# One issuing engine for the token transfers of the first unit, and a new hand-written order of 1382 steps, in a delta-rule attention + multiplicative FFN kernel

## The chip, the core and the metric

The kernel runs on one core of one Trainium2 chip. TensorE (PE) multiplies, VectorE (DVE), ScalarE (ACT) and GpSimd (POOL) do the elementwise work, SyncE (SP) issues nearly all transfers, and each engine runs its own instructions strictly in the order in which the program lists them. The metric is the device time of one execution in microseconds (us).

## The reference

```python
# q, k, v: (4, 8, 768, 48), beta: (4, 8, 768); w1, w2: (384, 1024), w3: (1024, 1024), w_out: (1024, 384)
k_n = k / (norm(k) + 1e-6);  state = 0
for t in range(768):
    y[:, :, t] = q_t @ state
    state += beta_t * outer(k_n_t, v_t - k_n_t @ state)
x = y as (4*768 tokens, 384)
out = ((x @ w1) * (x @ w2)) @ w3 @ w_out
```

## The kernel before, in words

The sequence is cut into 12 chunks `c` of 64 tokens; two chunks make a unit `u` (0 to 5), and one unit is 512 tokens over the four batches. The recurrence inside a chunk is solved with the inverse of a triangular 64x64 matrix, of which the two 32x32 diagonal blocks are inverted column by column on DVE. `w3 @ w_out` is folded into one matrix `w34` while the first unit is prepared, and the FFN of a unit runs on PE between the small products of the following chunks.

The program is written as generators; each `yield` ends a step. `ORDER` names one generator per word, and a word runs the next step of that generator. So the table alone sets the order of the instructions on every engine, across all parts. The generators that matter here:

- `k`, `q`, `v`: loads of a chunk. `g`, `N`: squares of the keys and their norms (`g` ends, and `N` ends, with a small product `across`, line 286, that swaps halves). `K`, `Q`: keys or queries transposed on PE (line 369) and copied to `KQ`.
- `s`: scores of a chunk (lines 409 for chunks 0 and 1, 451 and 457 later) and on DVE their products `U` and `PT`; `h`: query scores of chunks 0 and 1 (line 400); `u`: `U` sent to `Ud` in DRAM (line 491).
- `V0` to `V5`: the inversion for a unit. POOL clears `Vb`, the matrix `Ub` comes by a DVE transpose (unit 0, line 505) or from `Ud` (line 510); for units 0 and 1 ACT copies `Vb` in two halves into a PSUM tile `ps_w` (line 518); then come 31 steps of two DVE instructions (lines 524, 529). `V0` ends with four DVE transposes of 2 us (line 533).
- `e`: corner of the inverse (lines 563 to 646). `c`: the chain of chunk `c`, which is product, `R`, product, `X`, product, state `S` (PE line 672, DVE lines 706, 717, 738). `y`: outputs of a chunk (PE line 777), four ACT copies into `xT` (line 795), and the transfers of line 807 that lay the last heads over the free rows of `xT`.
- `P0` to `P35`: a piece of the weights: a transfer (line 837), two ACT conversions (845, 848), a DVE shift (850) and a POOL addition (852), which makes float32 out of float64. `t`: transpose of a piece of `w3` (PE 903, ACT 906); `f`: one fold (PE line 912, ACT 919) in two halves.
- `b` (first chunk of unit 0), `a` (the rest; `a02` is unit 0, column block 2): `x @ w1`, `x @ w2` (line 933), `ab` on ACT and DVE. `S`, `o`, `x`: sums, the last product (line 1165) and the results.

For the first unit the transfers of line 807 are issued per chunk: three for each half of the rows (`e` is 0 or 1). Those of `e == 1` are issued by ACT, all others by SP. An SP or ACT transfer waits for the landing of the eighth transfer before it, since eight completion semaphores go round.

Of the kernel before, what the change touches and what calls it, by code (L numbers as in the profile page):

```python
# [40 lines left out]
g0 N0 N0 P12 V0 P8 P8 P3 P3 P8 s1 P9 P9 Q1 s0 s0 P13 N0 P13 P3 P1 P9 t0 s1 s1 P0 P13 t4 V0 P1 V0
P2 P2 Q1 Q1 h1 P9 t4 P10 V0 P1 P3 P13 V0 P2 t5 P4 P6 V0 V0 P1 P2 t1 V0 P10 P10 P10 P4 P4 t0 V0
f0 V0 P5 V0 t2 P6 P5 P4 P6 P7 P5 t5 V0 P7 P7 P5 P7 f2 q0 t1 P18 V0 V0 V0 P11 P18 P18 V0 V0 P19
P6 P22 P18 f0 P11 P11 V0 P11 V0 f0 V0 V0 t2 f2 P19 P19 V0 t3 P16 f2 t3 P17 V0 t10 P22 P19 Q0 P23
t10 P16 f1 Q0 P22 f1 q2 P16 V0 V0 V0 Q0 P17 P17 P23 P23 f1 t11 V0 P17 t11 P23 P15 P14 h1 P15 q3
P21 f5 f5 P16 V0 V0 V0 V0 t8 f5 t8 h1 P20 P26 P22 t14 t14 h0 t9 P14 V0 V0 P15 P15 t7 t7 k2 V0
P21 t15 f4 t9 f4 P27 V0 V0 t15 v0 V0 P14 P14 t6 k3 Q2 V0 P26 t6 V0 f4 e0 P21 h0 P21 P28 f3 Q2 h0
e0 e0 e0 P20 K2 e1 e0 P26 P26 e0 Q2 g1 f7 n0 e1 e1 g1 g1 e0 g1 P27 P20 e1 n0 P28 P28 c0 c0 f7 e1
y0 g1 P25 P20 P29 v1 g1 g1 c0 y0 c0 P27 P27 n1 K2 K2 y0 y0 f3 f3 c1 P28 f7 n1 t12 K3 K3 t13 t12
f6 t13 P25 K3 P29 Q3 Q3 Q3 Q3 e1 e1 K2 P33 K2 P33 P25 g1 P25 g1 f6 c1 P24 c1 g1 N1 P33 c1 P33  # L50
P35 s2 P35 f6 P34 s2 s2 s2 P29 P29 s2 s2 P30 y1 y1 P34 s3 b6 b6 P34 P34 s3 P24 P35 s3 s3 Q3 P31
P31 b4 b4 s3 c1 u2 u3 N1 Q0 P35 P24 P24 y1 y1 b4 P30 V1 V1 c1 P31 b6 b6 N1 s3 k4 g2 b4 b3 b3 P32
P30 b5 b5 b5 b5 v2 P31 P30 V1 V1 a02 a04 V1 V1 V1 V1 b7 V1 V1 V1 V1 V1 b7 a04 a02 v3 a06 a06 V1
b1 b1 a07 a03 V1 V1 V1 V1 a03 V1 T T P32 c2 P32 P32 V1 k5 a01 a01 a07 V1 V1 a05 b0 n2 b0 a04 a04
V1 a02 a02 a05 V1 V1 T V1 b2 V1 V1 a07 b2 a07 V1 V1 a00 a03 a00 V1 V1 T V1 a03 V1 V1 a06 a00 a06
b3 b1 b3 a00 V1 b0 b1 g2 g2 g2 b0 S0 K3 a01 b7 n2 c2 g2 g2 g2 V1 K3 p4 b7 p4 V1 b2 b2 a05 a01 o0
x0 g2 e2 e2 e2 e2 e3 a05 d4 S0 n3 S0 d4 p5 S0 S0 o0 g2 e2 S0 o0 e3 e2 c2 c2 e3 e3 n3 o0 S0 c2 S0
g2 c2 e3 c3 e3 N2 c3 x0 x0 S0 Q1 S0 d4 S0 d4 o0 y2 p5 c3 S0 x0 o0 y2 V2 S0 c3 S0 y3 d5 d5 S0 y3
x0 x0 x0 x0 s4 s4 d5 d5 s4 s4 s4 s4 s5 s5 s5 s5 s5 s5 y3 S0 N2 u4 u5 c3 c3 x0 o0 x0 x0 a14 a14
a14 a17 a17 N2 a14 a15 a15 V2 V2 V2 V2 V2 V2 V2 V2 V2 a16 a13 a13 V2 V2 V2 V2 a16 V2 v5 V2 p6  # L60
a10 V2 a10 p6 V2 a11 V2 V2 a11 k7 V2 a12 V2 V2 V2 V2 a11 V2 V2 a10 a12 V2 V2 V2 v4 V2 V2 V2 a11
a10 S1 d6 d6 c4 k6 g3 g3 a12 a13 a12 d6 a15 a15 V2 e4 a17 e5 e4 e4 n4 n4 c4 g3 a16 p7 g3 g3 g3
a17 g3 d6 a13 e4 e4 g3 g3 g3 a16 S1 o1 e4 c4 e5 e5 p7 e5 o1 S1 c4 c4 c4 n5 S1 n5 e5 x1 N3 o1 S1
c5 S1 c5 e5 S1 y4 S1 k8 o1 y4 d7 d7 d7 S1 S1 S1 d7 x1 g4 s7 s7 s7 s7 s7 s7 N3 S1 S1 s6 s6 s6 s6
s6 S1 s6 g4 c5 x1 c5 u7 u6 V3 S1 o1 V3 x1 y5 y5 y5 o1 x1 x1 N3 c5 c5 x1 k9 x1 v7 V3 V3 V3 V3 V3
S1 o1 x1 x1 V3 V3 V3 V3 V3 x1 c6 V3 V3 a24 V3 V3 V3 V3 a24 a24 a24 V3 V3 a27 a27 a27 V3 V3 a27
a22 a22 a20 a22 V3 V3 p8 p8 V3 V3 g4 a22 V3 V3 a26 a20 V3 a20 V3 V3 V3 a26 V3 a26 a20 S2 a21 v6
n6 a26 g4 g4 g4 d8 d8 g4 g4 d8 a25 a25 a25 n6 a21 a21 V3 e6 e6 c6 a25 e6 d8 s8 g4 p9 e6 e6 e6 g4
N4 s8 s8 n7 a23 a23 e7 e7 p9 a21 S2 a23 e7 e7 c6 a23 o2 o2 e7 e7 x2 c6 y6 c6 S2 o2 x2 c6 y6 V4
S2 o2 c7 x2 d9 d9 d9 S2 d9 S2 S2 s8 n7 c7 c7 S2 S2 S2 S2 v8 s8 s8 S2 S2 o2 c7 y7 x2 u8 o2 s9 x2  # L70
x2 s9 y7 y7 s9 s9 s9 u9 x2 S2 S2 S2 o2 V4 v9 a30 c7 x2 x2 x2 N4 a31 a31 a30 a32 a32 N4 p10 V4 V4
p10 a35 V4 V4 V4 a36 V4 V4 V4 a33 a33 V4 V4 a37 V4 V4 V4 a36 V4 V4 V4 V4 V4 V4 x2 V4 V4 V4 n8
a35 V4 a34 a34 a34 a37 V4 a33 a31 V4 V4 V4 V4 V4 V4 V4 c7 k10 a34 d10 a33 k11 V4 e8 d10 a30 a30
S3 a36 a36 a31 a35 s9 e8 Q1 c8 g5 g5 g5 e8 e8 d10 a35 g5 n8 c8 a37 a37 e8 e9 e8 e9 a32 a32 e9 c8
g5 g5 g5 o3 e9 c8 n9 n9 p11 g5 g5 g5 v10 S3 S3 V5 e9 e9 c8 S3 S3 S3 o3 x3 o3 x3 x3 d10 c8 c9 c9
S3 S3 S3 y8 y8 c9 c9 o3 p11 s10 y9 N5 N5 o3 S3 S3 S3 S3 s10 S3 d11 d11 W s10 s10 x3 S3 o3 d11
d11 y9 y9 s10 s10 x3 x3 u10 x3 s11 s11 s11 s11 s11 S3 n10 x3 s11 o3 u11 a46 V5 v11 a46 x3 x3 c9
n10 a47 c9 W a47 N5 K0 a42 V5 V5 V5 V5 V5 V5 a42 a40 a40 V5 V5 a43 a44 a44 W Q0 V5 a41 a41 V5 V5
V5 V5 V5 V5 V5 V5 V5 V5 V5 V5 a45 a43 a45 V5 V5 V5 a44 a44 a43 V5 V5 V5 V5 V5 a45 a41 V5 V5 a41
a43 x3 a40 a45 a40 S4 S4 a42 a42 a46 c10 V5 e10 e10 e10 a47 c10 e10 e10 o4 e10 c10 e11 e11 a47  # L80
a46 K1 e11 o4 S4 S4 c10 S4 c10 S4 S4 S4 S4 c10 S4 x4 S4 e11 e11 e11 o4 W x4 n11 c11 n11 W y10
c11 S4 S4 S4 y10 o4 c11 o4 c11 y11 x4 x4 o4 x4 S4 S4 y11 x4 o4 y11 x4 x4 a50 x4 x4 a51 X5 X5 X5
a52 a50 a50 a50 a50 a50 a50 a50 a50 a50 a50 X5 a50 a50 a50 a50 a50 x4 a50 a50 a50 a51 a51 a50
a50 a51 a51 a51 a51 a51 a51 a51 a51 a51 a51 W a51 a51 a51 a51 a51 a51 a51 W a51 W a52 a52 a52
a52 a52 a52 a52 a52 a52 a52 a52 a52 a52 a52 a52 a52 a52 a52 a52 a53 a53 a52 a53 a53 a53 a53 a53
a53 a53 a53 a53 a53 a53 a53 a53 a53 a53 a53 a53 o5 x5 a53 a53 o5 o5 S5 S5 Q2 Q2 S5 o5 x5 x5 S5
o5 S5 S5 o5 S5 x5 S5 o5 x5 K0 x5 x5 x5 x5 x5 x5 K1 x5 x5 x5
"""


# [1 line left out]
def kernel(  # L92
# [651 lines left out]
    def outputs(c):  # L744
# [55 lines left out]
        if u == 0 or cc == 1:  # L800
            cs = slice(cc, cc + 1) if u == 0 else slice(0, 2)
            for e in range(2):
                dma = act.dma_start if u == 0 and e else sync.dma_start
                for j in range(KM):
                    g = C * e + D
                    s = C * e + 16 * j
                    dma(out=xT[g : g + 16, j, :, cs], in_=xT[s : s + 16, NP - 1, :, cs])
# [550 lines left out]
```

## Time and profile before

| | |
|---|---|
| time, median of 3 runs | 562.68 us (562.05 to 563.88) |
| the profiled execution, its own time | 564.32 us |
| its span, first to last instruction | 562.6 us |
| outside the span | 1.7 us |
| PE busy | 535.5 us, 95% |
| DVE, POOL, ACT busy | 342.8, 169.4, 145.7 us |
| mean granted TensorE clock | 0.993 |
| transfers | 54.21 MB, 96 GB/s over the span, 0.9 and more of the DMA engines' time in the first 60 us |

The profile is of one execution, read on one core. Busy time of PE counts a matmul from its start to a modelled end. An idle stretch is written in square brackets, with the event that ended it behind the arrow; "issue" there means that the engine waited for nothing that the profile shows. A matmul of float32 appears as two PE instructions.

### The profile page before, as it was taken

What the parts mean: (1) busy time and instruction counts of PE and PEld (TensorE: products, weight loads), DVE (VectorE), ACT (ScalarE), POOL (GpSimd) and SP (SyncE); (2) the same over time, 40 slices, a digit from 0 to 9 for tenths busy, and PEclk for the clock granted to TensorE, in tenths of its full rate; (3) what the DMA queues carried; (4) which work ended last, traced back from release to release, by engine and by line L of the source; (5) the groups of instructions that cost most, each with busy time, mean ns of one, the idle gap of its engine ahead of it and who ended that gap; (6) DMA issues with size and microseconds to landing.
All of it is one profiled execution on the core that took longest, in us unless ns stands there. A gap on an engine that the chain in (4) does not pass through costs nothing.

```text
span 562.6 us, 19911 instructions
## 1 busy us (share of the span) xinstructions
PE 535.5 (95%) x8732; PEld 392.9 (70%) x8732; DVE 342.8 (61%) x800; ACT 145.7 (26%) x291; POOL 169.4 (30%) x213
## 2 busy tenths in 40 slices
PE   5689999899999999999999999999999999989997
PEld 4556667788888644698544798444986447988897
DVE  6799746469727489555895543796364973213553
ACT  3577755432131020120011220111210202212210
POOL 6565443427370002450003430004640002722000
PEclk9999999799999999999999999999999999999999
DMA  9899957587433674543645314745325012010001
GB/s 200 303 297 244 154 115 158 110 152 90 91 48 62 133 103 95 79 75 83 133 62 105 47 34 83 136 96 86 58 43 123 26 53 42 19 57 1 0 2 56
DMA packets 191526, 54.21 MB, mean 96 GB/s; under 512 B 178928, under 2 KB 185072, under 8 KB 191440
## 3 DMA queue, kind: packets, MB, share of 16 engines
q1 hardware_dynamic: 188848, 52.46, 46.8%
q8 instruction: 68, 1.11, 0.9%
q10 hardware_dynamic: 2592, 0.49, 0.6%
q14 instruction: 18, 0.15, 0.1%
HBM read 41.78 MB, written 9.96 MB: 92 GB/s over the span
## 4 chain that ended last, share of the span: by engine, by line
PE 84%; DVE 10%; issue 4%; DMA 1%; ACT 1%; POOL 0%; ACTq 0%; DVEq 0%
PE ps_f L933 37%; PE ps_f L1165 20%; PE ps_w L672 6%; PE ps_w L777 5%; PE ps_f L1073 4%; PE ps_w L619 3%; PE ps_w L1073 2%; PE ps_f L912 2%; DVE tb L524 2%; DVE ps_w L529 2%; PE ps_w L451 1%; PE ps_f L369 1%; PE ps_w L457 1%; DVE TT L533 1%; DMA ktok<-in_k_dram 1%
## 5 line engine op out<-in xcount | busy, mean ns | idle before, releaser
L1006 POOL TENSOR_TENSOR ab<-ab 128x256 f32<-128x256 f32 x80 | 56.0, 728 | 204.5 <-DVE ab L949 199.0
L933 PE MATMUL ps_f<-xT,w1s 128*128 128x512 f32 (+1 forms) x288 | 108.3, 529 | 0.0
L933 PE MATMUL ps_f<-xT,w2s 128*128 128x512 f32 (+1 forms) x288 | 107.0, 523 | 0.0
L933 PEld LDWEIGHTS ps_f<-xT,w1s 128*128 128x128 f32 x288 | 54.8, 193 | 45.6 <-issue 41.1
L933 PEld LDWEIGHTS ps_f<-xT,w2s 128*128 128x128 f32 x288 | 54.2, 190 | 46.2 <-issue 42.8
L945 ACT COPY ab<-ps_f 128x512 f32<-128x512 f32 (+1 forms) x48 | 23.6, 516 | 137.8 <-PE ps_f L933 125.1
L1165 PE MATMUL ps_f<-w,ab 128*128 128x192 f32 x320 | 56.8, 331 | 1.8 <-DVE osb L1196 1.8
L1165 PEld LDWEIGHTS ps_f<-w,ab 128*128 128x128 f32 x320 | 51.6, 190 | 3.0 <-issue 2.1
L524 DVE TENSOR_TENSOR tb<-Vb,Ub 128x31 f32<-128x31 f32 (+15 forms) x124 | 43.1, 347 | 9.8 <-DMA Ub<-Ud 5.8
L912 PE MATMUL ps_f<-wo,w3T 128*128 128x384 f32 x128 | 43.8, 492 | 1.6 <-ACT w3T L906 1.6
L529 DVE TENSOR_TENSOR Vb<-Vb,tb 128x31 f32<-128x31 f32 (+15 forms) x124 | 42.5, 343 | 4.3
L1165 PE MATMUL ps_f<-room,ab 128*128 128x192 f32 x240 | 42.9, 332 | 0.2 <-ACT osb L1202 0.2
L949 DVE TENSOR_TENSOR ab<-ab,ps_f 128x512 f32<-128x512 f32 (+1 forms) x48 | 27.6, 589 | 22.9 <-PE ps_f L933 22.7
L1165 PEld LDWEIGHTS ps_f<-room,ab 128*128 128x128 f32 x240 | 38.6, 190 | 1.1 <-issue 0.3
L912 PEld LDWEIGHTS ps_f<-wo,w3T 128*128 128x128 f32 x128 | 23.4, 190 | 16.5 <-ACT w3T L906 1.8
L301 POOL TENSOR_TENSOR sq<-ktok 128x384 f32<-128x384 f32 x24 | 19.8, 834 | 49.4 <-DMA out_dram<-osb 24.6
L635 ACT COPY T<-ps_w 32x512 f32<-32x512 f32 x24 | 13.8, 575 | 71.6 <-PE ps_w L619 64.2
L795 ACT COPY xT<-ps_w 112x256 f32<-112x256 f32 x48 | 14.3, 384 | 64.5 <-PE ps_w L777 61.7
L1196 DVE TENSOR_TENSOR room<-room,ps_f 128x384 f32<-128x384 f32 (+1 forms) x13 | 7.0, 535 | 28.6 <-PE ps_f L1165 28.6
L451 PE MATMUL ps_w<-KQ 48*64 48x128 f32 x320 | 21.9, 281 | 2.0 <-DVE PT L474 1.4
L717 DVE TENSOR_TENSOR X<-ps_w,wt 128x768 f32<-128x768 f32 x12 | 11.5, 957 | 20.0 <-PE ps_w L672 17.6
L524 DVE TENSOR_TENSOR tb<-ps_w,Ub 128x31 f32<-128x31 f32 (+15 forms) x62 | 21.0, 339 | 4.2 <-ACT ps_w L518 1.6
(170 smaller groups left out, 806.8 us busy)
## 6 DMA issues: line engine op xcount, KB each, us to landing
vtok<-in_v_dram SPq DMA_DIRECT2D x24, 192.0 KB, 4.5
out_dram<-osb SPq DMA_DIRECT2D x23, 192.0 KB, 2.2
ktok<-in_k_dram SPq DMA_DIRECT2D x44, 96.0 KB, 3.6
raw<-in_moe_w_dram SPq DMA_DIRECT2D x8, 512.0 KB, 6.9
raw<-in_moe_w_dram SPq DMA_DIRECT2D x18, 192.0 KB, 4.8
raw<-in_moe_w_out_dram SPq DMA_DIRECT2D x7, 384.0 KB, 4.9
...
```

Of the source, the lines that this page charges most:

```text
L451: pe.matmul(ps[half(z), 0, n : n + 128], lhsT=x[:, 0, :], rhs=x.rearrange("p j t -> p (j t)"), start=True, stop=True,)
L524: dve.tensor_tensor(out=tv, in0=V[:, 0 : s + 1, s : s + 1].to_broadcast([P, s + 1, n]), in1=U[:, s, s + 1 : BS].unsqueeze(1).to_broadcast( ...
L529: dve.tensor_tensor(out=o, in0=o, in1=tv, op=ALU.subtract)
L672: pe.matmul(out(ps, r, h, z), lhsT=lhs(r, h, z), rhs=rhs(r, h, z), start=True, stop=True,)
L777: i = pe.matmul(region(h, z, r), lhsT=lhs, rhs=rhs, start=part[n] not in part[:n], stop=part[n] not in part[n + 1 :],)
L912: pe.matmul(ps[:, 0:DM], lhsT=w3Ts[jc, kc // 4][:, kc % 4 * P : kc % 4 * P + P], rhs=wo(kc), start=(kc == 0), stop=(kc == KF - 1),)
L933: pe.matmul(ps[:].rearrange("p b c t -> p b (c t)"), lhsT=w[:, m, js], rhs=x[:, m, :, c0:c1].rearrange("p b c t -> p b (c t)"), start=(m = ...
L945: act.copy(out=t, in_=ps)
L949: dve.tensor_tensor(out=t, in0=t, in1=ps, op=ALU.mult)
L1006: (dve if u == last else pool).tensor_tensor(out=o_, in0=x_, in1=y_, op=op)
L1073: pe.matmul(ps[:, j, :], lhsT=w[j], rhs=x, start=first and j == 0, stop=j == 1, skip_group_check=not first,)
L1165: pe.matmul(ps[b][:, b, :], lhsT=ab_of(u, HF * f + i, t0), rhs=ws_[w][:, i], start=first and i == 0 and (b == 0 or n == "F"), stop=i == HF ...
```

## The change

The first part: in the first unit the `e == 1` half of the transfers of line 807 (line 806 after) is issued by SP too. The second part: `ORDER` holds the same 1382 words in another order. No arithmetic, tile, buffer or shape is changed, but since buffers are taken in rotation, a step that comes earlier may take another one.

```diff
         if u == 0 or cc == 1:
             cs = slice(cc, cc + 1) if u == 0 else slice(0, 2)
             for e in range(2):
-                dma = act.dma_start if u == 0 and e else sync.dma_start
                 for j in range(KM):
                     g = C * e + D
                     s = C * e + 16 * j
-                    dma(out=xT[g : g + 16, j, :, cs], in_=xT[s : s + 16, NP - 1, :, cs])
+                    sync.dma_start(
+                        out=xT[g : g + 16, j, :, cs], in_=xT[s : s + 16, NP - 1, :, cs]
+                    )
                 if u == 0 or e:
                     yield
```

The first line of the table, before and after:

```diff
-k0 g0 k1 K0 K0 g0 P12 K0 g0 beta P0 g0 g0 g0 P8 K1 K1 g0 P12 g0 P12 P0 P0 q1 beta beta K1 g0 s0
+k0 g0 g0 g0 K0 V0 g0 k1 P12 K0 K0 beta K1 P0 g0 g0 K1 K1 g0 q1 P12 g0 P12 P12 beta g0 g0 beta N0
```

The first place is the start of PE's program. The rows are the transposes of the keys (line 369), `beta`, the small products of line 286 (`ss` from `g0`, `wt` from `N0`), the scores of chunks 0 and 1 (line 409), the queries, and the first transposes of `w3` (line 903, after the change 904). Before:

```order
L369 MATMUL ps_f<-ident,ktok 48x64 x64
L1257 MATMUL ps_f<-ident,beta_fm 128x16 x12
L286 MATMUL ps_f<-ss,ident 64x16 x2
L409 MATMUL ps_w<-KQ 32x64 x64
L286 MATMUL ps_f<-wt,ident 64x16 x2
L409 MATMUL ps_w<-KQ 32x64 x64
L369 MATMUL ps_f<-ident,X 48x2x32 x32
```

And in the same place after:

```order
L369 MATMUL ps_f<-ident,ktok 48x64 x64
L1258 MATMUL ps_f<-ident,beta_fm 128x16 x12
L286 MATMUL ps_f<-ss,ident 64x16 x2
L409 MATMUL ps_w<-KQ 32x64 x128
L369 MATMUL ps_f<-ident,X 48x2x32 x32
L904 MATMUL ps_f<-ident,w_276 128x128 x4
L904 MATMUL ps_f<-ident,w_289 128x128 x4
```

The product of `wt`, which needs the end of `N0` on DVE, no longer stands between the scores of the two chunks; it now follows the query scores and the third transpose of `w3`.

The second place is on ACT, where the two copies of `Vb` into `ps_w` (line 518) stand; `w3` and `wo` rows are weight conversions, `KQ` rows copies of queries, `w3T` rows copies of a transposed piece of `w3` (`w3T_564` before and `w3T_497` after are the first one that a fold needs). Before:

```order
L518 COPY ps_w_101<-Vb_342 128x512
L845 ACTIVATE wo_223<-spare_114 128x384
L848 ACTIVATE spare_114<-spare_114 128x384
L379 COPY KQ_182<-ps_f_99 112x8x64
L379 COPY KQ_182<-ps_f_93 112x8x64
L906 COPY w3T_522<-ps_f_97 128x512
L518 COPY ps_w_101<-Vb_342 128x512
L845 ACTIVATE w3_556<-kperm_91 128x512
L848 ACTIVATE kperm_91<-kperm_91 128x512
L845 ACTIVATE wo_223<-raw_537 128x384
L848 ACTIVATE raw_537<-raw_537 128x384
L906 COPY w3T_564<-ps_f_95 128x512
```

And after:

```order
L846 ACTIVATE w3_428<-raw_426 128x512
L849 ACTIVATE raw_426<-raw_426 128x512
L518 COPY ps_w_101<-Vb_162 128x512 x2
L846 ACTIVATE wo_283<-raw_438 128x384
L849 ACTIVATE raw_438<-raw_438 128x384
L379 COPY KQ_178<-ps_f_97 112x8x64
L379 COPY KQ_178<-ps_f_99 112x8x64
L846 ACTIVATE w3_487<-kperm_91 128x512
L849 ACTIVATE kperm_91<-kperm_91 128x512
L846 ACTIVATE wo_283<-spare_114 128x384
L849 ACTIVATE spare_114<-spare_114 128x384
L907 COPY w3T_497<-ps_f_93 128x512
```

The second copy now follows the first at once, ahead of the query copies and of every copy that waits for a transpose of `w3`.

The third place is SP's queue around the second chunk's transfers of line 807 (806 after). `Ud` is the store for the second inversion, `Ub` its load, `kperm<-in_moe_w2` the last weight piece. Before:

```order
L491 DMA Ud_1810<-U_106 32x16x32 x8
L807 DMA xT_1294<-xT_1294 16x4x64 x3
L510 DMA Ub_1838<-Ud_1810 128x1024
L233 DMA ktok_1850<-in_k_dram 64x8x48 x4
L837 DMA kperm_91<-in_moe_w2_dram 48x1024
L837 DMA kperm_91<-in_moe_w2_dram 16x1024
```

And after:

```order
L491 DMA Ud_1752<-U_106 32x16x32 x8
L806 DMA xT_1296<-xT_1296 16x4x64 x3
L510 DMA Ub_1842<-Ud_1752 128x1024
L806 DMA xT_1296<-xT_1296 16x4x64 x3
L838 DMA kperm_91<-in_moe_w2_dram 48x1024
L838 DMA kperm_91<-in_moe_w2_dram 16x1024
```

The three transfers that ACT issued now stand behind the load of `Ub`, which waits for the last `Ud` to land. The words of the table from the last half of `s3` on show what PE does meanwhile, up to `a02`, the first user of the second chunk's `xT` (in `b4 b4` the first word is PE's, the second ACT's, and so on):

```diff
-b4 b4 s3 c1 u2 u3 N1 Q0 P35 P24 P24 y1 y1 b4 P30 V1 V1 c1 P31 b6 b6 N1 s3 k4 g2 b4 b3 b3 P32 P30 b5 b5 b5 b5 v2 P31 P30 V1 V1 a02
+s3 s3 s3 Q0 P30 P30 c1 b4 b4 P24 P24 u3 P24 y1 b5 b5 b5 V1 P26 y1 V1 b5 P31 V1 P32 b6 b6 P31 b4 b0 b0 c1 b3 b4 b3 b7 V1 V1 b7 V1 V1 a02
```

More of the change, by code (lines that the diff above doesn't have):

```diff
@@ L39 @@
 ORDER = """
-k0 g0 k1 K0 K0 g0 P12 K0 g0 beta P0 g0 g0 g0 P8 K1 K1 g0 P12 g0 P12 P0 P0 q1 beta beta K1 g0 s0
[L41 to L87, printed above, removed]
+k0 g0 g0 g0 K0 V0 g0 k1 P12 K0 K0 beta K1 P0 g0 g0 K1 K1 g0 q1 P12 g0 P12 P12 beta g0 g0 beta N0
@@ new lines @@
+P8 P9 P8 P8 P8 P3 P0 P3 P3 P9 P0 s1 s1 s1 P9 s0 P3 P0 P13 P13 P13 s0 s0 V0 V0 V0 P1 P1 Q1 P1 P9
+Q1 P10 P13 V0 V0 Q1 P1 P10 P2 P2 t0 t0 P2 P4 P4 V0 t1 P2 t1 V0 P4 P4 h1 t4 t4 N0 P6 f0 P7 P10
+P10 P5 t2 t5 P18 V0 V0 P11 P6 V0 P6 P6 N0 P16 P19 V0 P7 P7 P5 P5 P5 q0 V0 t5 h1 P18 f2 P11 V0
+P18 P7 t2 V0 f0 P14 h1 P22 P18 P19 f0 V0 P11 V0 V0 P11 P19 V0 V0 V0 P16 P16 P17 f2 f2 t10 t10
+P23 Q0 Q0 t3 P19 t11 V0 P16 Q0 V0 t3 P22 P22 P22 P14 V0 V0 V0 f1 V0 V0 P23 P21 t8 P15 f1 P14 t11
+P17 P17 f5 f5 V0 V0 f1 V0 V0 P17 t8 P15 V0 h0 V0 V0 P14 f5 P26 t6 P23 P20 V0 q2 P27 k2 t6 t9 t14
@@ new lines @@
+t9 v0 V0 P23 f4 f4 t14 f4 t15 t15 P21 P15 P15 t7 q3 V0 v1 Q2 Q2 V0 e0 h0 h0 e0 Q2 g1 e0 g1 t7 g1
+f3 e0 e0 K2 P27 K2 e1 e0 e0 n0 e1 k3 f7 P27 n0 e1 c0 e1 P21 e1 f7 V1 g1 c0 y0 P28 c0 P20 P25 f7
+P20 P20 P29 f3 P33 y0 n1 n1 P21 g1 c0 c1 y0 g1 g1 K2 f3 P28 P28 P28 P34 c1 t13 t13 t12 t12 P25
+P27 K3 K3 K3 e1 s2 g1 P25 P29 P35 g1 P25 P33 f6 f6 P29 P29 e1 g1 N1 Q3 Q3 c1 y0 s2 s2 s2 P34 c1
+s2 s2 f6 Q3 s3 K2 P30 P34 P34 P26 P26 P24 y1 y1 s3 P30 P31 N1 P33 N1 s3 b6 b6 P33 P35 P35 u2 P35
+s3 s3 s3 Q0 P30 P30 c1 b4 b4 P24 P24 u3 P24 y1 b5 b5 b5 V1 P26 y1 V1 b5 P31 V1 P32 b6 b6 P31 b4
@@ new lines @@
+b0 b0 c1 b3 b4 b3 b7 V1 V1 b7 V1 V1 a02 V1 a02 V1 a03 V1 a05 V1 k4 V1 a00 V1 V1 P32 P32 a03 V1
+b1 a00 a05 V1 V1 V1 V1 a04 V1 b1 c2 P32 P31 a04 a04 a04 a01 a01 T T T v2 n2 a02 T V1 k5 a07 a07
+V1 v3 a02 V1 V1 a03 a03 V1 V1 V1 V1 V1 V1 a06 a06 b2 V1 b2 a07 a07 V1 a01 V1 V1 V1 a01 p4 p4 b2
+n3 V1 V1 b2 a00 a00 a05 a05 g2 g2 g2 g2 a06 n2 b1 b1 b0 e2 b0 a06 g2 b3 b3 b7 b7 o0 g2 c2 n3 x0
+e2 e2 g2 g2 o0 d4 e2 g2 e2 g2 o0 S0 S0 S0 e2 c2 d4 S0 S0 e3 S0 S0 x0 S0 S0 S0 S0 e3 e3 S0 S0 d4
+p5 c2 c2 e3 c2 x0 S0 o0 c3 S0 e3 c3 o0 e3 N2 y2 c3 x0 o0 d4 p5 y2 S0 c3 y3 x0 x0 x0 d5 d5 s4 s4
@@ new lines @@
+o0 x0 y3 s4 s4 d5 d5 s4 s4 N2 s5 y3 u4 s5 V2 s5 s5 s5 N2 s5 c3 u5 V2 x0 p6 x0 a14 p6 a14 a14 a14
+a13 a13 V2 V2 V2 V2 V2 a12 a12 V2 a16 a16 V2 V2 V2 V2 V2 V2 V2 a15 V2 a15 a11 a11 V2 V2 V2 V2 V2
+V2 V2 V2 V2 v5 x0 V2 a10 V2 V2 k6 V2 v4 V2 V2 V2 V2 a17 a17 a15 a15 a10 k7 d6 d6 d6 a10 a10 c3
+S1 n5 n4 a13 a12 a12 a13 V2 e4 a17 e4 a11 g3 g3 g3 g3 a11 Q3 c4 g3 g3 n4 c4 e4 a16 a16 e5 e4 e4
+e4 o1 x1 S1 a17 S1 S1 S1 e5 e5 S1 e5 d6 n5 g3 c4 c4 g3 o1 S1 c4 V3 c4 g3 e5 e5 o1 p7 g3 N3 c5 p7
+x1 S1 x1 S1 y4 S1 y4 c5 o1 d7 d7 d7 d7 s7 s7 k8 g4 s7 s7 s6 s7 s7 u7 s6 s6 s6 s6 s6 c5 S1 c5 o1
@@ new lines @@
+u6 y5 S1 x1 V3 o1 S1 x1 x1 c5 S1 y5 y5 S1 x1 V3 k9 S1 g4 c5 x1 x1 p8 V3 V3 V3 V3 V3 o1 c6 x1 V3
+V3 N3 N3 V3 V3 V3 V3 V3 V3 a27 a27 a25 x1 g4 a20 a25 a20 V3 V3 a25 a25 p8 a22 a22 V3 a24 a21 g4
+V3 V3 V3 a24 V3 d8 d8 p9 v6 V3 V3 a21 g4 g4 V3 V3 V3 V3 V3 V3 V3 V3 a22 a22 a27 a27 a20 n6 a20
+V3 e6 g4 a26 a26 a26 a24 d8 a21 n6 c6 e6 a26 d8 e7 a24 e6 e6 p9 g4 g4 g4 s8 N4 s8 a23 a23 s8 e6
+S2 e7 a21 e6 a23 a23 c6 e7 e7 c6 v7 o2 v9 o2 n7 n7 S2 y6 S2 S2 S2 V4 x2 K2 N4 c6 c6 o2 y6 e7 S2
+S2 S2 d9 d9 p10 S2 e7 c7 S2 x2 o2 d9 d9 c7 S2 s8 c7 x2 s8 o2 s8 c7 S2 y7 S2 v8 n8 x2 K1 o2 x2 x2
@@ new lines @@
+u8 Q2 s9 s9 S2 S2 s9 y7 y7 s9 s9 u9 S2 o2 x2 s9 c7 x2 c7 V4 a32 a32 N4 k10 x2 x2 a36 a36 d10 d10
+V4 a30 a30 V4 V4 a33 a35 Q1 V4 a37 V4 V4 V4 V4 a33 V4 V4 c8 V4 V4 V4 V4 a35 a37 V4 V4 V4 k11 a34
+n9 a34 a31 p10 V4 V4 V4 V4 a34 V4 V4 V4 V4 x2 V4 V4 V4 V4 V4 V4 V4 e8 a31 d10 a31 a31 a35 a34 V5
+a33 a30 a30 a36 n8 c8 K3 e8 e8 a35 a37 a33 a36 e8 K3 e8 e8 a37 a32 e9 e9 e9 p11 e9 c8 a32 o3 x3
+S3 S3 g5 g5 g5 g5 n9 g5 S3 c8 d10 S3 S3 S3 c8 e9 p11 g5 g5 g5 o3 o3 e9 c8 c9 x3 x3 S3 S3 g5 g5
+c9 y8 y8 K1 S3 S3 c9 c9 o3 N5 o3 x3 s10 d11 s10 s10 y9 s10 s10 d11 d11 d11 S3 S3 W y9 y9 S3 S3
@@ new lines @@
+o3 x3 W s10 x3 x3 s11 s11 s11 s11 s11 u10 u11 V5 S3 S3 x3 x3 o3 x3 x3 a44 s11 v11 V5 a45 V5 V5
+V5 V5 a45 a42 a42 v10 V5 a44 a46 a46 V5 V5 V5 V5 V5 V5 a41 V5 V5 V5 V5 a43 c9 a43 V5 V5 a41 a47
+a47 V5 V5 a44 a44 V5 V5 V5 V5 W V5 a40 a40 a45 V5 a43 V5 a41 V5 V5 V5 V5 a43 a45 a42 a40 a42 c9
+a46 V5 e10 e11 e10 W a41 W a40 c10 n10 n10 c10 e10 N5 a47 e10 e10 W a46 S4 a47 S4 S4 o4 S4 S4 S4
+e10 e11 e11 W x4 e11 c10 o4 S4 N5 e11 c10 c10 e11 c10 S4 S4 o4 x4 y10 S4 c11 n11 o4 S4 y10 n11
+c11 c11 c11 S4 S4 o4 y11 x4 S4 y11 y11 S4 x4 o4 S4 x4 x4 x4 x4 x4 o4 x4 a50 a50 a51 X5 a52 X5
@@ L88 @@
+a50 X5 W a50 a50 a50 X5 a50 a50 a50 a50 a50 a50 a50 a50 a50 a50 a50 Q0 a50 a50 a50 a51 a51 a50
+a51 a51 a51 a51 a51 a51 a51 a51 a51 a51 a51 a51 a51 a51 a51 a52 a51 a51 a51 a52 a52 a52 a52 a52
+a52 a52 a52 a52 a52 a52 a52 a52 a52 a52 a52 a52 a52 a52 S5 a53 a53 a53 a53 a53 a53 a53 a53 Q3
+a53 a53 a53 a53 a53 a53 a53 a53 a53 a53 a53 a53 o5 x5 a53 S5 S5 o5 o5 S5 S5 o5 S5 S5 x5 o5 o5 K0
+S5 o5 x4 Q2 x5 x5 x5 x5 x5 x5 x5 x5 x5 x5 x5 x5 K0 Q1
 """
```

## The prediction

> **What bounds the kernel now.** The page's busy times say which engine to follow, then busy time and granted clock were read by stage.
>
> ```profile
> PE 535.5 (95%) x8732; PEld 392.9 (70%) x8732; DVE 342.8 (61%) x800; ACT 145.7 (26%) x291; POOL 169.4 (30%) x213
> ```
>
> The windows below have, from the left, the stretch, its length, busy time of PE, PEld, DVE, ACT and POOL, then the granted clock, the DMA engines' share and GB/s.
>
> ```profile
> 0.00:40.00 40.00, 26.67 (x580) 20.62 (x581) 31.15 (x80) 23.21 (x44) 24.79 (x36) 1.00 0.93 264
> 40.00:105.00 65.00, 61.61 (x1398) 43.22 (x1396) 41.89 (x91) 41.53 (x80) 26.83 (x24) 0.97 0.86 175
> 105.00:155.00 50.00, 50.00 (x453) 43.18 (x453) 37.74 (x99) 13.47 (x31) 24.38 (x27) 0.97 0.62 101
> 155.00:503.00 348.00, 340.71 (x6016) 234.37 (x6017) 207.16 (x491) 57.33 (x121) 86.82 (x121) 1.00 0.41 75
> 503.00:562.60 59.60, 56.49 (x290) 51.48 (x288) 24.89 (x40) 10.13 (x18) 6.60 (x8) 0.99 0.06 21
> ```
>
> PE is idle 13.3 us in the first 40, 3.4 in the next 65, 7.3 in the long stretch from 155 and 3.1 at the end: 27.1 in all. Its work is the same after the change, so the time moves only by that idle time and by stretches at a lower clock, which stand between 40 and 155 (0.97). The start is the largest. What PE waited for there (in total, times, longest):
>
> ```profile
> PE ps_f L369 <- DMA ktok<-in_k_dram: 5.5, 2, 4.7
> PE ps_w L409 <- issue: 2.9, 2, 1.6
> PE ps_f L286 <- DVE wt L334: 1.8, 1, 1.8
> PE ps_f L912 <- ACT w3T L906: 1.6, 1, 1.6
> ```
>
> The first is the keys' transfer, which nothing in the change brings sooner. The other three lie where PE's order is changed.
>
> **The change part by part: the start.** After the change the scores of chunk 1 follow those of chunk 0 directly, and the second copy of `Vb` follows the first. The first inversion needs three things in turn, seen on DVE's timeline (start, duration):
>
> ```profile
> 22.59 1.29 DVE L420 TENSOR_TENSOR U<-ps_w,wt 128x512 f32<-128x512 f32 x2 [1.19 <-PE ps_w L409]
> 24.12 2.01 DVE L505 STREAM_TRANSPOSE Ub<-U 128x1024 f32<-128x1024 f32 x1
> 27.98 0.19 DVE L524 TENSOR_TENSOR tb<-ps_w,Ub 128x31 f32<-128x31 f32 x1 [1.63 <-ACT ps_w L518]
> ```
>
> and on ACT's:
>
> ```profile
> 21.73 0.58 ACT L518 COPY ps_w<-Vb 128x512 f32<-128x512 f32 x1
> 26.87 0.58 ACT L906 COPY w3T<-ps_f 128x512 f32<-128x512 f32 x1 [1.31 <-PE ps_f L903]
> 27.35 0.60 ACT L518 COPY ps_w<-Vb 128x512 f32<-128x512 f32 x1
> ```
>
> The second copy (27.35) stands behind a `w3T` copy that waits for PE, and DVE loses 1.63 us to it. In its new place it follows the first one, at 22 to 23 us, and that wait ends. What is late next on DVE is its own queue. The score wait of 1.19 (and of PE's 1.8 for `wt`) shrinks too; I take 0.9 to 1.5 of it, so the transpose starts at 22.6 to 23.2 instead of 24.12 and ends 2.0 later; the weight shifts that stand in between, now behind ACT's conversions, give back 0.35 to 0.55. Line 524 starts at 25.6 to 26.0 instead of 27.98: 2.0 to 2.4 us earlier. PE has the other side of the start:
>
> ```profile
> 30.50 2.85 PE L912 MATMUL ps_f<-wo,w3T 128*128 128x384 f32 x8 [1.56 <-ACT w3T L906]
> ```
>
> The first fold came only with its `w3T`, behind ACT's queue, in which one `w3T` copy (0.58) and the wait of 1.31 now stand elsewhere: 1.9 together, so 28.6. Both queues meet at the end of the inversion, where DVE's transposes release PE:
>
> ```profile
> 60.46 4.01 DVE L533 STREAM_TRANSPOSE TT<-ps_w 32x1024 f32<-32x1024 f32 x2
> ...
> 64.52 0.63 PE L563 MATMUL ps_w<-TT,ident 32*32 32x256 f32 x8
> ```
>
> The transposes end at 64.47 and the corner begins at 64.52, so only what both gain passes on: 1.9 at most. The last `wo` conversions wait for loads, with the DMA engines at 0.93 of their time, and come no earlier; a fold that meets them gives back up to 0.7. The gain is 1.2 to 1.9, and I take **1.7**, near the upper end since only the last of many conversions is exposed. If the loads carry all of it the term is 0; if all of DVE's gain passed it would be 2.4.
>
> **The hole at 99 to 107.**
>
> ```profile
> 101.22 0.88 PE L777 MATMUL ps_w<-PT,X 64*48 64x64 f32 x22 [1.91 <-issue]
> ```
>
> ```profile
> 101.00:107.00 6.00, 5.69 (x107) 5.00 (x107) 1.86 (x3) 2.31 (x6) 1.25 (x1) 0.50 0.68 137
> 107.00:108.00 1.00, 1.00 (x15) 0.39 (x17) 0.92 (x2) 0.15 (x1) 0.64 (x2) 0.68 0.08 16
> ```
>
> ```profile
> q8 instruction: 68, 1.11, 0.9%
> ```
>
> PE stops for 1.91 us in the middle of 64 like products that wait for no data, and then runs at clock 0.50 from 101.2 and 0.68 to 108: 5.8 x 0.5 + 0.3 = 3.2 us of work lost, 5.1 with the stop. The likely cause is the supply of instructions: the instruction queue moved 1.11 MB in 68 packets, 16.3 KB each, or one for 257 of PE's 17,464 rows (8732 products and as many weight loads), and the DMA engines are full here:
>
> ```profile
> 84.00:88.00 4.00, 4.00 (x140) 3.37 (x140) 0.69 (x1) 1.98 (x5) 2.95 (x4) 1.00 0.21 58
> 88.00:92.00 4.00, 4.00 (x140) 2.89 (x139) 2.14 (x5) 3.71 (x8) 1.31 (x1) 1.00 0.96 201
> ...
> 100.00:104.00 4.00, 2.69 (x82) 2.48 (x85) 0.00 (x0) 0.79 (x4) 0.00 (x0) 0.60 0.96 204
> ```
>
> From 88 they are busy with the last weights, before that nearly idle. The new order issues those loads earlier against PE's program, and puts the same outputs `y1` behind two folds, so the burst still lies before `y1`, and longer. The event costs 5.1 again or nothing. I take no change, as the burst and the run of small products both remain, and keep 0 and -5.1 as ends. The Trainium skill ("Runtime: NRT & Kernel Launch", Instruction fetch mechanics) has instructions refilled in 16 KiB blocks of 256, mostly hidden; the block size agrees with the queue's row, the 1.91 us does not look hidden. By that rule nothing would come from moving the loads. The Trainium skill ("TensorE: Matmul & The Clock Gate", Part 1) lets the clock fall to half after about 3.4 us without work, in a window that runs free. Here an idle of 1.91 was followed by 0.50; by the rule the clock loss could go or come by chance, and 1.9 of the 5.1 would be the stop's own.
>
> **The transfers of the first unit.** Issue times, and from issue to landing (minimum, median, maximum), of line 807 on both queues and of line 491:
>
> ```profile
> L807 SPq DMA_DIRECT2D xT<-xT x6: 585/636/1498, 81.6 to 115.2; - x6
> L807 ACTq DMA_DIRECT2D xT<-xT x6: 593/618/844, 81.6 to 111.8; - x6
> DMA to landing us min/median/max: 1.8/2.2/3.4
> ```
>
> ```profile
> L491 SPq DMA_DIRECT2D Ud<-U x8: 302/314/497, 101.8 to 112.8; - x8
> DMA to landing us min/median/max: 2.0/2.7/4.6
> ```
>
> ```profile
> 101.78 11.30 SPq L491 DMA_DIRECT2D Ud<-U  x8
> 113.19 2.59 SPq L807 DMA_DIRECT2D xT<-xT  x3
> 115.96 0.44 SPq L510 DMA_DIRECT2D Ub<-Ud  x1
> ```
>
> ACT is rid of six issues of 0.62, two times 1.9 us. It is busy 13.5 of 50 us there, so that brings nothing to PE. SP gets six more. The second three are behind the `Ub` load in the new order, and that load waits until `Ud` has landed. From the end T of the scores of chunk 3, `U` takes DVE 1.3 (the 1.29 of line 420). Four of the eight `Ud` go out beside it and four behind it, at 0.31 each, to T+2.6; the first three transfers, 0.64 each, to T+4.5; `Ub` waits for the landing of the last `Ud`, 2.7 after T+2.6, and takes 0.44, to T+5.7; the last three are issued by T+7.7 and landed 2.2 later, at T+9.9. If all eight `Ud` come behind `U`, everything from there is 1.2 later: T+11.1. The reader is the block `a02`. Now:
>
> ```profile
> 108.91 1.49 PE ps_f L933 x6
> 110.40 0.87 PE ps_w L672 x64
> ...
> 111.36 15.74 PE ps_f L933 x72
> ```
>
> 72 products of line 933 take 15.74, a half block of 6 takes 1.31. The new order has the product for the state (0.87) and eight such halves between T and `a02`: 0.87 + 10.48 = 11.35. So the transfers land 0.2 to 1.5 us ahead of their reader: cost 0, covered by those eight halves. The cover is thin. Before, T was 108.9 (the first row above), and the last `Ud` was issued at 112.8, 3.9 later, where my walk has 2.3 (T+2.6 less 0.31): 1.6 of lateness, for lanes whose earlier transfers had not landed. With the slowest landing, 4.6 instead of 2.7, it is 3.5. No gain is possible, as no product of line 933 waits for a transfer now.
>
> **The steady stretch and the end.** The largest wait from 155 on, the duration of `X` in the list of groups, and the corner product of chunk 2 in the chain:
>
> ```profile
> PE ps_f L1165 <- DVE osb L1196: 1.8, 2, 1.3
> ```
>
> ```profile
> L717 DVE TENSOR_TENSOR X<-ps_w,wt 128x768 f32<-128x768 f32 x12 | 11.5, 957 | 20.0 <-PE ps_w L672 17.6
> ```
>
> ```profile
> 154.28 0.69 PE ps_w L619 x52
> ```
>
> In chunk 2 only the corner product of 0.69 (line 619) now hides the 0.96 of `X`, so 0.3 to 0.6 comes; a last product behind `osb` may add 0.3 to 0.5; the 1.3 of before, which stood behind another queue, may go. I take 0, between +1.5 and -1.5.
>
> Sum: -1.7 + 0 + 0 + 0. The profiled execution took 564.32, 1.64 above the median of 562.68, with a span of 562.6 and 1.7 around it; it becomes 562.6, the span 560.9, and the median **561.0**.
>
> **The rivals.** *The hole closes.* If the earlier loads leave the DMA engines free when `y1` is fetched, stop and half clock go: 561.0 - 5.1 = 555.9. For it: 84 to 88 shows engines at 0.21 shortly before, so a few microseconds decide. Against: two more folds before `y1` only move the fetch along with the loads. With the stop alone gone it is 559.1.
>
> *The transfers wait (slower).* The last `Ud` lands late, `Ub` stands in SP's queue ahead of three transfers, and `a02` stops PE. It decides from the point at which the last `Ud` lands later than T+6.8 (11.35 less 2.2 for landing, 1.9 for three issues and 0.44). A lateness of 1.6 stops PE by 0.2 to 1.4, within the forecast's range. At 3.5 the transfers land at T+13.4 to T+14.6, a stop of 2.0 to 3.3: 563.0 to 564.3. The clock halved behind a stop of 1.91, so the 3.2 of that is added, 566.2 to 567.5, and I take **567**. For it: SP's `Ud` were late before, behind other landings. Against: fewer weight loads are left in the rotation at that time in the new order.
>
> *The start is not shortened.* The loads at 0.93 or the last conversions set the end of the folds: 562.7; or the gain is lost and the new order adds a stop like the 1.91 elsewhere, 564.6. For it: DMA is the fullest resource of the first 40 us. Against: the two waits that go are not for DMA.
>
> **How the numbers follow.** A measurement of this kernel tells 0.3%, 1.7 us. The forecast has 0.34 (own range 559.3 to 563.0: the term of the start at 1.2 to 1.9 and the steady stretch at up to 1.5 either way; 0.19 of it faster by over 0.3%, 0.13 within, 0.02 slower), the closed hole 0.25, all faster, the waiting transfers 0.25 (0.04 within, 0.21 slower), the start not shortened 0.16 (0.03 within, 0.13 slower). Faster: 0.19 + 0.25 = 0.44; within: 0.13 + 0.04 + 0.03 = 0.20; slower: 0.02 + 0.21 + 0.13 = 0.36. The range, 555 to 568, holds 555.9 and 567.5, so the 2 in 10 left out are mishaps on top of these cases.
>
> **What would show it.** The start is right if line 524 first starts at 25.6 to 26.3, the first fold at 28.6 and the corner product of line 563 at about 62.8. The hole is right if PE shows an "issue" wait of about 2 us at `y1` and a clock near 0.5 behind it; a full clock to 155 means the first rival. The transfers are right if no product of line 933 waits for `xT`; a wait for DMA at `a02` means the second. From 155 to 503 the idle time should be 6 to 9 us. The prediction is wrong if the first fold is not earlier, if the hole is another one, or if the long stretch holds a new wait of more than 2 us.

## The result, and the profile after

The changed kernel takes 557.18 us, the median of 4 executions (556.76 to 557.83); the kernel before took 563.28 beside it (562.05 to 566.10). The ratio is 0.989, interval 0.9865 to 0.9915: faster by 1.1%, some 6 us, where 1.7 were forecast. The profiled execution took 557.83 with a span of 556.1. Its windows, with the columns of those before:

```profile
0.00:40.00 40.00, 28.41 (x584) 21.29 (x585) 31.16 (x84) 25.21 (x47) 25.88 (x36) 1.00 0.93 276
40.00:105.00 65.00, 63.25 (x1519) 44.97 (x1518) 45.70 (x97) 41.00 (x79) 27.72 (x26) 1.00 0.78 168
105.00:155.00 50.00, 50.00 (x426) 44.41 (x425) 35.74 (x95) 13.67 (x30) 29.43 (x35) 1.00 0.61 105
155.00:503.00 348.00, 342.36 (x5952) 234.75 (x5951) 207.10 (x489) 57.44 (x120) 86.64 (x118) 1.00 0.42 75
503.00:556.10 53.10, 49.55 (x257) 45.35 (x256) 24.00 (x39) 8.38 (x15) 0.00 (x0) 1.00 0.05 15
```

PE is idle 11.6, 1.75, 0, 5.6 and 3.55 us, 22.5 in all against 27.1. By stages that is 1.7 less at the start, 1.6 less from 40 to 105, 1.65 less in the long stretch, 0.4 more at the end. The clock column reads 1.00 down to the end, and PE's busy time is 1.9 shorter (533.57 against 535.48) for the same work. Together 6.5, the difference of the two spans. Of the 1.7 at the start 1.1 is no gain: the wait for the keys is 1.2 shorter (4.3 against 5.5), but PE is then busy 1.1 longer with them, and the `beta` product behind them starts at 10.89, before at 10.88. From there on PE's busy time is 3.0 shorter, 0.8 of it up to the first corner and 2.2 behind it, where before lost its clock.

The start, on DVE's timeline and on PE's:

```profile
22.48 1.29 DVE L420 TENSOR_TENSOR U<-ps_w,wt 128x512 f32<-128x512 f32 x2 [0.42 <-PE ps_w L409]
23.80 2.04 DVE L505 STREAM_TRANSPOSE Ub<-U 128x1024 f32<-128x1024 f32 x1
25.97 0.18 DVE L524 TENSOR_TENSOR tb<-ps_w,Ub 128x31 f32<-128x31 f32 x1
```

```profile
28.05 2.85 PE L913 MATMUL ps_f<-wo,w3T 128*128 128x384 f32 x8 [0.43 <-ACT w3T L907]
63.02 0.63 PE L563 MATMUL ps_w<-TT,ident 32*32 32x256 f32 x8
```

The inversion starts 2.0 earlier and without a wait, the first fold 2.45 earlier, and the corner, where both meet, 1.5 earlier. PE has done the same products by then in both kernels (80 of the folds and 56 of the transposes of `w3` among them), so the start is worth 1.5 at this point. The place of the hole, on PE's timeline and in windows:

```profile
98.13 0.27 PE L777 MATMUL ps_w<-KQ,S 48*48 48x64 f32 x3 [0.53 <-issue]
```

```profile
92.00:96.00 4.00, 3.57 (x192) 3.23 (x194) 3.45 (x8) 2.90 (x6) 0.00 (x0) 1.00 0.64 162
96.00:100.00 4.00, 3.29 (x177) 2.86 (x168) 3.09 (x7) 0.83 (x2) 2.26 (x2) 1.00 0.91 200
100.00:104.00 4.00, 3.67 (x129) 2.96 (x122) 1.42 (x4) 3.74 (x9) 0.36 (x2) 1.00 0.59 113
```

The stop in `y1` has shrunk from 1.91 to 0.53, the clock stays full, and the DMA engines are no longer at their limit throughout. The two largest waits of PE over the span of after (total, times, longest):

```profile
PE ps_w L409 <- issue: 5.4, 2, 4.4
PE ps_f L369 <- DMA ktok<-in_k_dram: 4.3, 2, 4.1
```

No product waits for `xT`.

### The profile page after: what moved, and what is told of

It reads as the page before. It is cut to its first block, busy times and chain, and to the rows that moved or that the text cites. A ratio compares the mean times of both kernels' runs of the same rounds, so it can differ in the third digit from the quotient of the medians.

```text
span 556.1 us, 19932 instructions
## 1 busy us (share of the span) xinstructions
PE 533.6 (96%) x8732; PEld 390.8 (70%) x8732; DVE 343.7 (62%) x800; ACT 145.7 (26%) x291; POOL 169.7 (31%) x213
## 4 chain that ended last, share of the span: by engine, by line
PE 93%; DVE 3%; issue 2%; DMA 2%; ACT 0%; SPq 0%; DVEq 0%
PE ps_f L934 38%; PE ps_f L1166 20%; PE ps_f L913 7%; PE ps_w L672 6%; PE ps_w L777 4%; PE ps_f L1074 4%; PE ps_w L619 3%; PE ps_w L1074 2%; PE ps_w L451 2%; PE ps_f L369 1%; PE ps_w L457 1%; PE ps_f L904 1%; DMA beta_fm<-in_beta_dram 1%; PE ps_w L409 1%; PE ps_w L1166 1%
## 5 line engine op out<-in xcount | busy, mean ns | idle before, releaser
L934 PE MATMUL ps_f<-xT,w1s 128*128 128x512 f32 (+1 forms) x288 | 106.7, 524 | 0.0
L658 POOL TENSOR_TENSOR vtok<-vtok,n 128x384 f32<-128x384 f32 x24 | 19.8, 832 | 39.5 <-DMA vtok<-in_v_dram 39.5
L795 ACT COPY xT<-ps_w 112x256 f32<-112x256 f32 x48 | 14.3, 384 | 65.0 <-PE ps_w L777 61.7
```

Of the source, the lines that this page charges most:

```text
L934: pe.matmul(ps[:].rearrange("p b c t -> p b (c t)"), lhsT=w[:, m, js], rhs=x[:, m, :, c0:c1].rearrange("p b c t -> p b (c t)"), start=(m = ...
```

## The experiments

My theory after the result: the order alone brings the gain, in parts that add up (start, the hole with its clock, the long stretch), and the issuing engine is worth nothing. Times below are medians of 12 executions, except where a count is given. The kernel before ran beside them 110 times, with a median of 562.6.

One thing about these executions is needed to read them. The mean granted clock of each is taken as the sign that PE lost its clock around `y1`: it is then 0.991 to 0.997. Of the 14 kernels with a profile 13 agree with this; in `small_loads` such a mean comes from another place. In the executions without a profile the place is not shown. Another loss, seen at 13 to 27 us in three profiles, takes the mean down by a further 0.012 and occurs in about half of the executions of most kernels. It costs nothing: before has 562.6 with it (57 executions) and 562.65 without (53). The loss at `y1` costs 1.7 in before: of its 110 executions 64 have it, median 563.6, and 46 keep the clock, median 561.9. It is not a fixed price: in `sp_only` below six executions with it and six without differ by 0.1.

**Each half of the change alone.**

```diff
-the order before, e == 1 issued by ACT
+order_only: the new order, e == 1 still issued by ACT
+sp_only:    the order before, e == 1 issued by SP
```

> The new order, with the e == 1 transfers of the first unit still issued by ACT. Theory (the order alone brings the gain: 1.5 us at the start, some 4 at the hole of y1, the rest in the long stretch; the issuing engine is worth nothing): 557.2 us within 1, no stop of over 1 us at y1, clock 1.00 from 40 to 155. Rival (ACT, rid of six issues, is what frees the conversions and so the loads): 559 us or more, with part of the hole back.

> The old order, with all transfers of the first unit issued by SP. Theory (the order alone brings the gain): as before, 563.3 us within 1, with the stop of about 1.9 us at y1 and the clock at half after it. Rival (the issuing engine closes the hole): 559 us or less. Third possibility (SP's queue is what delays): 565 us or more, with a product of line 933 waiting for xT.

The order alone gives 564.88, ratio 1.0034 (1.0009 to 1.0059): slower than before. SP alone gives 563.52, ratio 1.0017 (0.9996 to 1.0038), which can't be told from no change; in its profile the stops at `y1` are shorter (1.2 the longest) and the clock stays full there. So the theory fell: under the new order the issuing engine is worth 7.7 us (564.88 less 557.18), under the old one nothing. The waits of SP's queue and of PE in the run of the order alone, from 80 us on:

```profile
SPq L837 <- DMA xT<-xT: 8.3, 1, 8.3
SPq L491 <- DMA xT<-xT: 3.3, 2, 2.7
```

```profile
PE ps_w L451 <- ACT KQ L379: 2.6, 1, 2.6
PE ps_f L933 <- ACT ab L945: 1.4, 1, 1.4
```

and ACT's timeline there, with a window of the same time:

```profile
92.84 0.59 ACT L379 COPY KQ<-ps_f 112x512 f32<-112x512 f32 x1 [3.47 <-PE ps_f L369]
92.85 2.97 ACTq L807 DMA_DIRECT2D xT<-xT  x3
96.00 0.67 ACT L845 ACTIVATE w2s<-qperm 128x512 f32<-128x512 f32 x1 [2.57 <-issue]
...
97.48 0.60 ACT L379 COPY KQ<-ps_f 112x512 f32<-112x512 f32 x1
```

```profile
92.00:96.00 4.00, 3.07 (x172) 2.70 (x162) 3.49 (x8) 0.59 (x1) 0.00 (x0) 1.00 0.07 14
```

The new order has a copy of transposed queries (`Q3`) ahead of the three transfers of chunk 0 in ACT's queue. That copy waits for PE until 92.84. A weight load in SP's queue, which has nothing to do with `xT`, needs the completion semaphore that one of these transfers uses: in the trace the eight that go round over both queues have the numbers 100 and 102 to 108, ACT's first transfer at 92.85 sets number 104, and SP's load waits for 104. So SP stands still for 8.3 us and the DMA engines with it (0.07 of their time, against 0.64 in the changed kernel). ACT is then held 3 us by its own transfers, the next copy of `KQ` comes at 97.48, and PE waits 2.6 for it. With all six in SP's queue no queue waits for another there: in the changed kernel SP has issued the same three by 90.9.

```profile
89.04 1.88 SPq L806 DMA_DIRECT2D xT<-xT  x3
```

**Which of the six.**

```diff
-dma = act.dma_start if u == 0 and e else sync.dma_start
+first_on_act:  dma = act.dma_start if u == 0 and e and cc == 0 else sync.dma_start
+second_on_act: dma = act.dma_start if u == 0 and e and cc == 1 else sync.dma_start
```

> The new order; of the first unit's e == 1 transfers only those of chunk 0 are issued by ACT, those of chunk 1 by SP. Theory (the completion semaphores are shared, so a transfer that stands late in ACT's queue holds up the weight loads in SP's; in the run with all six on ACT, SP waited 8.3 us for the three of chunk 0): most of the loss comes back, 562 to 564 us, SP waiting about 8 us for xT, and PE over 2 us for a copy of KQ. Rival (ACT's own issue time or the transfers of chunk 1 matter): 558 us or less.

> The new order; only those of chunk 1 are issued by ACT. Theory (shared semaphores, chunk 0 at fault): 557 to 559 us, with a wait of SP for xT of about 3 us at the stores of Ud. Rival: 561 us or more.

Measured: 560.75 and 561.36, 3.6 and 4.2 above the changed kernel, together the 7.7 of all six. The expectation that chunk 0 is most of it missed for both runs, and the second is at its rival's time; each half has its own way of holding up SP. With the first alone and with the second alone, SP's queue waited:

```profile
SPq L837 <- DMA xT<-xT: 9.1, 2, 8.5
```

```profile
SPq L491 <- DMA xT<-xT: 7.2, 2, 6.4
```

With the first, PE waits 2.7 for `KQ` and loses the clock at `y1` in 10 of 12 executions. With the second, the stores of `Ud` are late (the fourth waits for number 107, which ACT's first transfer sets), and PE waits 1.3 for `ab` on ACT and 0.8 on DVE, with the clock kept in 11 of 12.

**The stop at `y1` and the clock.**

```diff
 small_loads, on the kernel before, pieces 24 and 30 to 35:
-out=raw[rows, 0:n], in_=src
+out=raw[rows, 0:n // 8], in_=src[:, 0:n // 8]
 after_stop, on the changed kernel, second half of PT of chunk 2:
-dve.tensor_tensor(out=by_parity(PT), ...)
+for again in range(5): dve.tensor_tensor(out=by_parity(PT), ...)
```

> The kernel before, with the last seven weight pieces (24, 30 to 35) loaded as an eighth of their columns, which the conversions repeat; the FFN's weights are then not the reference's. Theory (the stop at y1 is PE's instructions coming late because the DMA engines are full): no issue wait over 0.7 us and no half clock between 95 and 108, 558.5 to 560.5 us. Rival (the stop comes with the run of small products, whatever the transfers): issue waits of 1.5 us or more at line 777 remain and the time is 562 to 564 us.

> The changed kernel with the DVE product that makes the second half of PT of chunk 2 (line 474) done five times instead of once: it adds 2.7 us to a wait of 0.43 that PE has there, a little before y1. Theory (a stop of 2 us or more there lets the clock fall to half for some 6 us in most executions, as in before): the wait is about 3.1 us, and the time 2.7 us above the changed kernel, with 2 us more in those executions whose mean clock is 0.997 or less apart from the start, which should be over half. Rival (a stop alone costs its own length): 2.7 us and no more, and no execution with that clock.

With the loads cut, before takes 559.62, ratio 0.9938 (0.9915 to 0.9960). From 80 to 110 PE waits once, 0.2 us, and the DMA engines are busy 0.19 of the time from 80 to 105:

```profile
80.00:105.00 25.00, 24.51 (x748) 18.55 (x740) 15.08 (x37) 14.09 (x34) 10.48 (x9) 1.00 0.19 38
```

So the stop goes when the load on the DMA engines goes, as the theory had it. Their load is not the whole of it: in `late_old` below they are full from 96 to 100 (1.01 in the share column), and PE has no such stop. That it is the fetch of instructions which comes late is argued from the block size; no run shows the fetch itself. A lost clock is still seen in 4 executions; in the one with a profile it begins at 176 to 180, at another place.

The added stop came at `y1` itself. On PE's timeline, and in the window behind it:

```profile
100.29 1.10 PE L778 MATMUL ps_w<-KQ,S 48*48 48x64 f32 x32 [2.85 <-DVE PT L475]
```

```profile
100.00:104.00 4.00, 3.59 (x132) 3.38 (x132) 2.42 (x6) 0.00 (x0) 2.63 (x2) 0.57 0.73 98
```

The time is 561.47, 4.3 above the changed kernel. All 12 executions lost the clock; of the changed kernel's 10 executions (below) none did. PE's waits from 85 to 112 are 3.1 in all, against 1.2 and 0.7 in the two profiles of the changed kernel; these 1.9 to 2.4 and the 1.7 that a lost clock costs in before make 3.6 to 4.1, near the 4.3. A stop of that length here sets the clock loss off, and it need not be an "issue" wait: this time PE waited for DVE.

**The changed kernel again, and its table in pieces.** The old and the new table hold the same steps, so the first part of one can be followed by what is left of the other. The cuts are at the first corner (224 steps before, 223 after) and at the chain of chunk 2 (419 and 415).

```diff
+start_new: new start, then the old order (e == 1 on ACT)
+mid_new:   old start, new middle, old rest
+late_new:  old start, old middle, new rest
+late_old:  new start, new middle, old rest
+start_old: old start, then the new order
```

> The changed kernel itself, in the same session as the two below and with more executions. If the four executions of it were typical: 557.2 us within 1, a ratio of 0.99 to before, and no execution with the clock lost at y1 (mean clock 0.997 or 0.994, or 0.985 or below). If they were lucky: 558.5 us or more with a spread like the other variants'.

> The new order's first 223 steps (up to the corner of the first inversion), then what is left in the old order; e == 1 on ACT. Theory (start and hole are separate terms): the corner at 63.0 instead of 64.5, the stop and the half clock at y1 as before, 561.8 us. Rival (the hole depends on when y1 meets the loads, and the earlier start alone moves it): no hole, 558 us or less; or the start's gain is lost again at a longer hole, 563.3.

> The old start (224 steps), the new order from there to the chain of chunk 2, the old order after that; all transfers on SP. Theory (three separate parts: start 1.5 to 2.6, the middle with the lost clock 1.5 to 2.5, the long stretch and what stands before it about 2): only the middle's gain is left, 560.5 to 562 us, with the lost clock in few executions. Rival (the middle is worth nothing by itself): 562.8 us, and the lost clock in two of three executions.

> The old order up to the chain of chunk 2 (first 419 steps), then what is left in the new order; all transfers on SP. Theory (the part from chunk 2 on is worth 2.8 to 4.3 us by itself, as the runs with old start and new middle and with new start and middle say): 559 to 561 us, with the old kernel's issue waits at y1 and a lost clock in about half of the executions. Rival (it needs the new middle before it): 562.5 us or more.

> The new order up to the chain of chunk 2 (first 415 steps), then what is left in the old order; all transfers on SP. Theory (the long stretch is worth its idle time, 7.3 against 5.6 us): 558.8 us. Rival (the long stretch is worth nothing, all of the gain lies before chunk 2): 557.2. Second rival (most of the gain lies there): 560 us or more.

> The old order's first 224 steps, then what is left in the new order; all transfers on SP. Theory (separate terms): the corner at 64.5, no hole, 558.7 us. Rival (the earlier start closed the hole): the stop and the half clock at y1 return, 562 us or more.

The values that `late_new` returns are not the reference's, probably since the bank of PSUM that holds the first product of `a07` comes round to `a00` before it is copied; the instructions are the same in kind and size.

| new parts | median | clock lost | median with the clock kept | PE idle 0-40, 40-105, 155-503 in the profile |
|---|---|---|---|---|
| none (before, on ACT) | 562.6 | 64 of 110 | 561.9 | 13.3, 3.4, 7.3 |
| none, on SP (`sp_only`) | 563.5 | 6 of 12 | 563.5 | 13.5, 2.5, 7.15 |
| start (on ACT) | 562.0 | 7 of 12 | 560.9 | 11.4, 4.7, 6.6 |
| middle | 562.6 | 6 of 12 | 562.0 | 11.75, 2.9, 7.6 |
| rest | 563.1 | 7 of 12 | 561.7 | 11.9, 3.8, 5.6 |
| start, middle | 561.5 | 4 of 12 | 560.9 | 12.3, 1.8, 6.9 |
| middle, rest | 559.8 | 1 of 12 | 559.7 | 14.3, 2.1, 5.9 |
| all, 4 executions | 557.2 | 0 of 4 | 557.2 | 11.6, 1.75, 5.6 |
| all again, 6 executions | 557.1 | 0 of 6 | 557.1 | 11.1, 1.2, 5.0 |

The changed kernel's time holds: ratio 0.9898 (0.9861 to 0.9935). In the profiles each stage follows its own part of the table. Line 563 starts at 63.6 to 64.8 in the six kernels with the old start and at 62.4 to 63.5 in the eight with the new one. The long stretch has 5.0 to 5.9 of idle time with the new rest and all transfers on SP, 6.6 to 7.6 with the old rest. Of the expectations those of `after_again` and `start_new` came out. `start_old` was 1.1 slower than expected, with issue waits of 1.2 and 0.6 about `y1` but the clock kept; `mid_new`, `late_new` and `late_old` missed too, and each is near its slower rival.

The medians do not add up. The rows on SP are to be read against `sp_only`, which differs from them by the order alone. The middle by itself brings 0.9, the rest 0.4, both 3.7, and all three 6.4 (in different sessions, in which before had medians of 562.25 to 563.0, so the 0.4 is not clear of noise). The start brings 1.1 before the new middle (561.5 against 562.6) and 2.7 before the new middle and rest (557.1 against 559.8); alone it was run on ACT, where it brings 0.6. The lost clock is part of it, since in this table it is rare (0 or 1 of 12 or fewer) only where middle and rest are both new. With the clock kept, middle and rest bring 1.6 and 1.8 alone and 3.8 together, which would add up, but these are medians of 5 and 6 executions that lie 2 to 3 us apart, and the rest still brings 3.8 behind the two other parts. Cut tables also have waits of their own: with the new middle and the old rest PE waits 0.7 for `ab` on DVE between 105 and 155, and neither before nor the changed kernel has that wait (`sp_only` has 0.4). Why a part is worth more with the others in place stays open.

## Why the prediction was right or wrong

**Direction and range:** right. 557.2 lies in 555 to 568, but below the forecast's own range (559.3 to 563.0); the time is nearest to that of the first rival (555.9), which had 0.25, and the sign named for that rival, a full clock to 155, is there. That the number comes so near is partly luck: the rival had nothing for the long stretch, where 1.65 of idle time went.

**The start:** right in its times, with one step wrong. Line 524 at 25.97 (forecast 25.6 to 26.0) with the wait of 1.63 gone, the fold at 28.05 (28.6), the corner at 63.02 (62.8). The term of 1.7 measured 1.5 there. The wrong step is that "the score wait of 1.19 (and of PE's 1.8 for `wt`) shrinks too" by 0.9 to 1.5. The wait for `wt` went, but PE's "issue" wait in the scores grew from 2.9 to 5.4 in its place, and the transpose of `U` began 0.3 earlier (23.80; forecast 22.6 to 23.2). The 0.35 to 0.55 that weight shifts were to give back did not come either, so the two errors nearly cancelled. Added up as they stand, the steps give 25.2 to 26.0 for line 524. What the start is worth in the end depends on the other parts: 0.6 alone, 1.1 and 2.7 in front of them.

**The hole:** wrong in the value taken. The step that failed is "I take no change, as the burst and the run of small products both remain". The burst remained, but it was weaker: 2.59 MB in the 16 us from 84 to 100, where before moved 3.12 MB from 88 to 104. The size was off too. The 5.1 came from one profiled execution with a clock loss of 3.2; over 110 executions the loss costs 1.7 and occurs in 64, so at the median of before it holds 0.7. The clock's rule that I cited from the Trainium skill ("TensorE: Matmul & The Clock Gate", Part 1), half rate after about 3.4 us without work, does not agree with these runs: 1.91 us and 2.85 us were enough here. A stop of 4.4 us at 17 to 21 us of the changed kernel's start left the clock at 1.00; that alone would not speak against the rule, since a window that runs free need not lie wholly in a stop of that length. That the stop shrank because the burst was weaker is argued: `small_loads` shows that the stop goes with the loads taken away, `late_old` that full DMA engines do not always make one.

**The transfers:** no wait at `a02`, as forecast, but only just. The last three were issued from 109.0 to 111.5 and took 2.9 to 4.3 to land, where the walk had 2.2, and eight halves of `b` after the chain of chunk 1 end at about 114.6. What failed is the sentence that relieving ACT "brings nothing to PE". It was costed under the old order, where it holds (563.5 against 562.6). Under the new order the same six issues on ACT cost 7.7. The step that was missing is that the completion semaphores tie the two queues together (SP stood still for 8.3 us behind ACT's transfer): the question was not what ACT saves but which of SP's loads stands behind a transfer that ACT has not reached. The Trainium skill ("DMA: Bandwidth & Descriptors", Issuing engines are not separate DMA queues) says that issuing on several engines saves only the time of issuing; here, in the new order, it cost 7.7 us.

**The long stretch:** a size was off. Term 0 within 1.5; the idle time fell by 1.65, to 5.6, below the 6 to 9 that were named as the sign. The `X` wait of chunk 2 came, 0.5 of the 0.3 to 0.6 forecast; a second wait for `osb` (0.5) and one of 0.5 for `S` went.

**The sum:** the terms were added as independent. The runs in pieces show that they are not, so even right terms would have given a wrong total.
